# The last four rows of a weight load: one 128-partition DMA, or sixteen of eight partitions

## The chip, the cores and the metric

The kernel runs on one core of a Trainium2 chip. The metric is the device time of one execution in microseconds (us). Before the change it is 186.64 us, the median of three runs (186.52 to 186.93).

## What is computed

One step of attention for 32 sequences, each with one new token, over a cache of which only the last 512 positions are read. There are 32 query heads and 8 key and value heads, each of 128 elements; everything is bf16.

```
q = (x @ wq), reshaped to [32 sequences, 32 heads, 128]          # x 32x512, wq 512x4096
k, v = the last 512 positions of k_cache, v_cache, each head used by 4 query heads
p = softmax(q . k * 128**-0.5)
o = p . v
out = o, reshaped to [32, 4096], @ wo                            # wo 4096x512
```

What has to come from memory is 75.5 MB: wq (4 MB), the windows of both caches (32 MB each, counted in units of 1024 x 1024 bytes) and wo (4 MB).

## The kernel before

The 32 sequences are worked on in eight groups q = 0 to 7 of four. A group's keys (4 MB) and values (4 MB) lie in SBUF across all 128 partitions; there are two buffers for each, `K_sb` and `V_sb`, used in turn. For each group VectorE turns the keys (`T`, L441), TensorE makes the scores (`S`, L331), ScalarE and VectorE the softmax, TensorE multiplies with the values (`P`, L361), and a few small steps bring the result into `o_sel`, the left operand of the output product (`C`, `F`, `D`). The orders of these steps on TensorE, VectorE and ScalarE are written out by hand (L19 to L33).

SyncE (SP) issues all loads but that of x, in the order of `LOADS` (L35): keys and values of the groups, the values of the last three groups in two, two and four pieces (`V_PIECES`, L40), and then wo in three pieces W0, W1 and W2. Four small DMAs for x, of 2, 6, 10 and 14 partitions (`X_PARTS`, L39), are issued by ScalarE at the start (L187).

wo is seen as 128 partitions of 32 rows: partition p holds rows 32p to 32p+31 of the 4096 x 512 matrix, 32 KB in one run in memory. It goes into the buffer of `K_sb[0]`, which is free once VectorE has turned the keys of group 6 (the wait at L240). The pieces are cut along the 32 rows (`WOP`, L41): W0 has rows 0 to 15 of every partition (16 KB each), W1 rows 16 to 27 (12 KB each), W2 rows 28 to 31 (4 KB each, 512 KB in all). Each piece has a semaphore of its own, `sem_wo[j]`, and a DMA adds 16 to it when it is done.

At the end TensorE waits for the last `D` step, and then goes through the pieces in order (L386 to L395): it waits for piece j, and does four matmuls (32 x 128) for each of its rows: 64 for W0, 48 for W1, 16 for W2. All accumulate in one bank, `Y_ps`. VectorE and ScalarE bring that to SBUF (L475, L524), and SP, which has waited for both, issues the one DMA of the output (L248).

Of the kernel before, what the change touches and what calls it, by code (L numbers as in the profile page):

```python
# [38 lines left out]
X_PARTS = [(0, 2), (2, 8), (8, 18), (18, 32)]  # L39
V_PIECES = [1, 1, 1, 1, 1, 2, 2, 4]  # L40
WOP = [(0, 16), (16, 28), (28, 32)]  # L41


def ops_of(text):
    return [(w[0],) + tuple(int(n) for n in w[1:].split(".")) for w in text.split()]


def bass_standalone__sliding_block_cached__sampling_kernel(
# [7 lines left out]
):  # L56
    B, Sq, D = x.shape
    _, HKV, SK, DH = k_cache.shape
    HD = wq.shape[1]
    HQ = HD // DH  # L60
# [3 lines left out]
    P = 128  # L64
# [55 lines left out]
    with ExitStack() as es:  # L120
# [26 lines left out]
        wo_sb = K_sb[0][:, :].rearrange("p (i n) -> p i n", i=NI)  # L147
# [20 lines left out]
        sem_v = [[sem(f"sem_v{i}_{j}") for j in range(max(V_PIECES))] for i in range(2)]  # L168
        sem_wo = [sem(f"sem_wo{i}") for i in range(len(WOP))]
        sem_out = sem("sem_out")  # L170
# [20 lines left out]
        def load_wq(i):  # L191

            nc.sync.dma_start(
                wq_sb[:, 2 * i:2 * i + 2, :].rearrange("p k n -> p (k n)"),
                wq.rearrange("(p k) n -> p k n", k=DKT)[:, 2 * i:2 * i + 2].rearrange("p k n -> p (k n)"),
            ).then_inc(sem_wq[i], 16)
# [4 lines left out]
        def rows(cache, q, r0=0, r1=R):  # L201
            return cache[4 * q:4 * q + 4, :, SK - W:, :].rearrange(
                "b h (k r) d -> (b h) k (r d)", k=KB)[:, :, r0 * DH:r1 * DH]
# [14 lines left out]
        @block.sync  # L218
        def _(sp):
            wait = Waits(sp)  # L220
            load_wq(1)
            wo_r = wo.rearrange("(p i) n -> p i n", i=NI)
            for op in ops_of(" ".join(LOADS)):
                kind, q = op[0], op[1]
                if kind == "K":
                    if q >= 2:
                        wait([ends["T", q - 2, 1]])
                    sp.dma_start(K_sb[q % 2][:, :], rows(k_cache, q)).then_inc(sem_k[q % 2], 16)
                elif kind == "V":
                    if q == 1:  # L230
                        sp.wait_ge(s["pe_q"], 8)
                    if q >= 2:
                        wait([ends["P", q - 2, 31]])
                    n = R // V_PIECES[q]
                    r0 = op[2] * n
                    sp.dma_start(  # L236
                        V_sb[q % 2][:, r0 * DH:(r0 + n) * DH], rows(v_cache, q, r0, r0 + n)
                    ).then_inc(sem_v[q % 2][op[2]], 16)
                else:
                    wait([ends["T", NQ - 2, 1]])  # L240
                    i0, i1 = WOP[q]
                    sp.dma_start(  # L242
                        wo_sb[:, i0:i1, :].rearrange("p i n -> p (i n)"),
                        wo_r[:, i0:i1, :].rearrange("p i n -> p (i n)"),
                    ).then_inc(sem_wo[q], 16)
            sp.wait_ge(s["dve_y"], 2)
            sp.wait_ge(s["act_y"], 2)
            sp.dma_start(  # L248
                out.rearrange("b s n -> b (s n)"), out_sb[:, :, :].rearrange("b c n -> b (c n)")
            ).then_inc(sem_out, 16)  # L250
            sp.wait_ge(sem_out, 16)
# [44 lines left out]
        def _(pe):  # L296
# [87 lines left out]
                run[op[0]](*op[1:]).then_inc(op_sem["PE", op[0]], 1)  # L384
            wait([ends["D", NQ - 1]])
            for j, (i0, i1) in enumerate(WOP):  # L386
                pe.wait_ge(sem_wo[j], 16)
                for i in range(i0, i1):
                    for c in range(4):
                        ins = pe.matmul(  # L390
                            Y_ps[32 * c:32 * (c + 1), 0:P],
                            lhsT=o_sel[:, i, :],
                            rhs=wo_sb[:, i, c * P:(c + 1) * P],
                            start=i == 0, stop=i == NI - 1, tile_position=(0, 32 * c),
                        )  # L395
# [159 lines left out]
```

## Time and profile before

| | us |
|---|---|
| median of three runs | 186.64 |
| the profiled execution's own time | 186.46 |
| span of its profile, first to last instruction | 184.7 |
| VectorE busy | 106.5 |
| TensorE matmul busy | 120.1 |
| ScalarE busy | 49.8 |
| SP issues W0, W1, W2 at | 158.04, 158.69, 159.19 |
| the last TensorE matmul of the kernel ends at | 182.08 |

Times within the profile count from the start of the span, which is 1.76 us shorter than the execution it belongs to. A core's DMAs are carried by 16 DMA engines, and each load by all of them or some of them. A row of a load that lies in one run in memory is one packet in the trace; after the last row that an engine carries of a DMA it writes one packet of 4 bytes, here called a mark, which adds 1 to the DMA's semaphore. The trace has the start and the length of every packet, without the number of its engine, and the time at which every increment of a semaphore landed. Over the span the DMA engines moved 410 GB/s, and the page's row of DMA shares stands at 9 tenths or more from the second of its 40 slices to the 38th.

### The profile page before, as it was taken

How to read it: one execution, taken by the hardware profiler on the slowest of the kernel's cores; microseconds unless marked ns; L12 is line 12 of the kernel's file. 1: busy time of each engine (PE TensorE's matmuls, PEld its weight loads, DVE VectorE, ACT ScalarE, POOL GpSimd, SP SyncE). 2: the span in 40 equal slices, each digit the busy share in tenths (PEclk: the TensorE clock that was granted, in tenths of full speed). 3: DMA queues.
4: the chain of work that ended last, by engine and by line, in shares of the span. 5: the costliest groups of instructions: out<-in, count | busy, mean ns of one | idle time of the engine just before them, and what ended most of it. 6: DMA issues, size and time to landing. Idle time of an engine off the chain costs nothing.

```text
span 184.7 us, 3664 instructions
## 1 busy us (share of the span) xinstructions
PE 120.1 (65%) x1636; PEld 56.9 (31%) x1636; DVE 106.5 (58%) x106; ACT 49.8 (27%) x93; POOL 16.9 (9%) x52
## 2 busy tenths in 40 slices
PE   0089304436599795749944992441899799898942
PEld 0024100013344451403521350000345345354541
DVE  0030999996469632963298327999746996311201
ACT  3000400010952357101650162001072804511211
POOL 7900040201000100002000200010000000000000
PEclk9999955555879999555999699555589999999998
DMA  6999999999999999999999999999999999999970
GB/s 220 411 497 405 405 454 454 447 397 405 451 454 451 390 401 454 454 444 405 392 451 454 440 397 412 454 433 440 415 412 422 419 429 426 410 419 433 425 305 31
DMA packets 3872, 75.80 MB, mean 410 GB/s; under 512 B 464, under 2 KB 528, under 8 KB 656
## 3 DMA queue, kind: packets, MB, share of 16 engines
q1 hardware_dynamic: 3792, 75.53, 96.1%
q8 instruction: 13, 0.21, 0.5%
q10 hardware_dynamic: 64, 0.03, 0.1%
q14 instruction: 3, 0.02, 0.0%
HBM read 75.53 MB, written 0.03 MB: 409 GB/s over the span
## 4 chain that ended last, share of the span: by engine, by line
DMA 59%; DVE 22%; PE 10%; issue 6%; SPq 2%; ACTq 1%; DVEq 0%
DMA K_sb<-in_k_cache_dram 43%; DVE KT_sb L441 16%; DMA K_sb<-in_wo_dram 12%; PE ps L313 4%; PE ps L361 4%; DMA bd<-in_x_dram 4%; DVE QT_sb L433 2%; DVE KT_sb L430 1%; SPq L236 1%; DVE C_sb L466 1%; ACTq L187 1%; SPq L242 1%; PE ps L331 1%; DVE bd L409 0%; PE ps L301 0%
## 5 line engine op out<-in xcount | busy, mean ns | idle before, releaser
L441 DVE STREAM_TRANSPOSE KT_sb<-K_sb 128x4096 f32<-128x4096 f32 x16 | 70.5, 4430 | 10.5 <-DMA K_sb<-in_k_cache_dram 10.4
L361 PE MATMUL ps<-V_sb,bd 32*128 32x512 bf16 x1024 | 63.9, 401 | 4.2 <-DMA V_sb<-in_v_cache_dram 1.6
L331 PE MATMUL ps<-KT_sb,QBD 128*32 128x512 bf16 x256 | 25.1, 529 | 37.3 <-DVE KT_sb L441 28.1
L361 PEld LDWEIGHTS ps<-V_sb,bd 32*128 32x128 bf16 x1024 | 27.3, 98 | 38.5 <-issue 14.9
L331 PEld LDWEIGHTS ps<-KT_sb,QBD 128*32 128x32 bf16 x256 | 6.6, 113 | 52.7 <-DVE KT_sb L441 34.1
L492 ACT ACTIVATE P_f<-ps,negmax 128x512 f32<-128x512 f32 x8 | 5.5, 685 | 60.6 <-DVE negmax L449 60.6
L505 ACT ACTIVATE bd<-PTc,mask 128x512 bf16<-128x512 bf16 x31 | 20.1, 710 | 0.3
L510 ACT ACTIVATE C_sb<-ps 32x512 f32<-32x512 f32 x22 | 12.9, 588 | 25.2 <-PE ps L361 25.1
L289 POOL COPY QBD<-QT_sb 32x128 bf16<-32x128 bf16 x32 | 9.2, 287 | 106.8 <-PE ps L331 89.2
L461 DVE TENSOR_SCALAR bd<-PTc,mask 128x512 bf16<-128x512 bf16 x33 | 9.4, 349 | 14.2 <-ACT PTc L499 14.2
L466 DVE COPY C_sb<-ps 32x512 f32<-32x512 f32 x10 | 6.9, 693 | 14.5 <-PE ps L361 14.3
L373 PE MATMUL ps<-C_sb,F_sb 128*128 128x128 f32 x64 | 10.1, 306 | 7.1 <-ACT C_sb L510 6.5
L373 PEld LDWEIGHTS ps<-C_sb,F_sb 128*128 128x128 f32 x64 | 8.6, 208 | 10.0 <-ACT C_sb L510 8.7
L346 PE MATMUL ps<-P_bf,E_sb 128*128 128x128 bf16 x128 | 10.1, 243 | 0.8 <-DVE P_bf L455 0.8
L313 PE MATMUL ps<-V_sb,bd 128*128 128x512 bf16 x32 | 9.8, 480 | 0.8 <-DVE bd L409 0.8
L346 PEld LDWEIGHTS ps<-P_bf,E_sb 128*128 128x128 bf16 x128 | 8.6, 110 | 4.9 <-DVE P_bf L455 2.8
L447 DVE TENSOR_REDUCE maxv<-ps 128x1 f32<-128x512 f32 x8 | 5.5, 687 | 7.8 <-PE ps L331 7.7
L499 ACT ACTIVATE PTc<-ps 128x512 bf16<-128x512 f32 x8 | 4.8, 594 | 18.5 <-PE ps L346 18.4
L430 DVE CAST KT_sb<-ps 128x512 bf16<-128x512 f32 x4 | 2.5, 684 | 7.3 <-PE ps L313 7.3
L301 PE MATMUL ps<-bd 32*128 32x128 bf16 x4 | 0.6, 295 | 9.0 <-DMA bd<-in_x_dram 9.0
L409 DVE CAST bd<-ps 128x512 bf16<-128x512 f32 x1 | 0.7, 691 | 9.6 <-PE ps L301 9.6
L486 ACT ACTIVATE KT_sb<-ps 128x512 bf16<-128x512 f32 x4 | 2.1, 602 | 15.1 <-PE ps L313 15.1
(29 smaller groups left out, 34.1 us busy)
## 6 DMA issues: line engine op xcount, KB each, us to landing
K_sb<-in_k_cache_dram SPq DMA_DIRECT2D x8, 4096.0 KB, 25.4
V_sb<-in_v_cache_dram SPq DMA_DIRECT2D x5, 4096.0 KB, 29.6
V_sb<-in_v_cache_dram SPq DMA_DIRECT2D x4, 2048.0 KB, 20.5
V_sb<-in_wq_dram SPq DMA_DIRECT2D x2, 2048.0 KB, 9.8
V_sb<-in_v_cache_dram SPq DMA_DIRECT2D x4, 1024.0 KB, 11.6
K_sb<-in_wo_dram SPq DMA_DIRECT2D x1, 2048.0 KB, 18.6
K_sb<-in_wo_dram SPq DMA_DIRECT2D x1, 1536.0 KB, 21.7
K_sb<-in_wo_dram SPq DMA_DIRECT2D x1, 512.0 KB, 22.4
```

The costliest lines, as they stand in the source:

```text
L289: pool.tensor_copy(QBD[pr, q % 2].rearrange("p (w t) (h c) -> p w t h c", w=2, h=HKV)[:, :, :, :, 4 * b:4 * b + 4], QT_sb[pr, q].rearrange ...
L313: ins = pe.matmul(ps[:, n], lhsT=xT_sb[:, kt, :], rhs=wq_sb[:, kt, n * 512:(n + 1) * 512], start=kt == 0, stop=kt == DKT - 1, tile_positio ...
L331: ins = pe.matmul(S_ps[32 * c:32 * c + 32, :], lhsT=QBD[:, q % 2, 2 * w + t, c0:c0 + 32], rhs=KT_sb[:, w, :, KB * h:KB * h + KB, t], start ...
L346: ins = pe.matmul(EP_ps[:, e * R:(e + 1) * R], lhsT=E_sb[:, k, e].rearrange("p m j -> p (m j)"), rhs=P_bf[:, k * R:(k + 1) * R], start=k = ...
L361: ins = pe.matmul(O_ps[:, b, :], lhsT=bd[pr, q % 2, 4 * g:4 * g + 4].rearrange("p r h e -> p (r h e)"), rhs=V_sb[q % 2][pr, 512 * g:512 * ...
L373: ins = pe.matmul(F_ps[:, 0:P], lhsT=F_sb[:, d].rearrange("p h d -> p (h d)"), rhs=C_sb[:, q % 2, :, 32 * d:32 * d + 32], start=d == 0, st ...
L441: return dve.transpose(KT_sb[:, w].bitcast(F32).rearrange("p r c t -> p r (c t)"), K_sb[q % 2][:, :].bitcast(F32).rearrange("p (r w c) -> ...
L447: dve.tensor_reduce(maxv[:, q:q + 1], S_ps, AX.X, ALU.max).then_inc(s["dve_m"], 1)
L461: ins = dve.tensor_scalar(o, i, m, None, op0=ALU.mult)
L466: ins = dve.tensor_copy(*pick_args(q, r))
L505: ins = act.activation(o, i, ACTF.Copy, scale=m)
L510: ins = act.activation(*pick_args(q, r), ACTF.Copy)
```

## The change

W0 and W1 are left as they are. W2 no longer comes by one DMA of 128 partitions but by 16 DMAs of eight partitions: DMA (g, r), with g and r from 0 to 3, takes partitions 32g+r, 32g+r+4, ... 32g+r+28. They are issued by SP in the place of the one DMA, in the order of g and then r, so the first eight cover partitions 0 to 63 and the last eight partitions 64 to 127. Each adds 16 to the same semaphore, and TensorE waits for 256 on it rather than for 16. The bytes, their places and TensorE's work are the same.

```diff
 WOP = [(0, 16), (16, 28), (28, 32)]
+
+WO_ROWS = [128, 128, 8]
...
                     i0, i1 = WOP[q]
-                    sp.dma_start(
-                        wo_sb[:, i0:i1, :].rearrange("p i n -> p (i n)"),
-                        wo_r[:, i0:i1, :].rearrange("p i n -> p (i n)"),
-                    ).then_inc(sem_wo[q], 16)
+                    n = WO_ROWS[q]
+
+                    for p0, step in [(0, 1)] if n == P else [
+                            (32 * g + r, P // (4 * n)) for g in range(4) for r in range(4)]:
+                        pr = slice(p0, p0 + step * (n - 1) + 1, step)
+                        sp.dma_start(
+                            wo_sb[pr, i0:i1, :].rearrange("p i n -> p (i n)"),
+                            wo_r[pr, i0:i1, :].rearrange("p i n -> p (i n)"),
+                        ).then_inc(sem_wo[q], 16)
...
             for j, (i0, i1) in enumerate(WOP):
-                pe.wait_ge(sem_wo[j], 16)
+                pe.wait_ge(sem_wo[j], 16 * (P // WO_ROWS[j]))
```

## Prediction

> **What bounds the kernel now.** I first read the page's DMA part and the end of the chain of waits, because the change touches only the last load. The chain, whose columns are start, length and what, ends so:
>
> ```profile
> 159.19 22.41 DMA K_sb<-in_wo_dram
> 181.60 0.04 issue
> 181.64 0.44 PE ps L390 x16
> 182.08 0.02 issue
> 182.10 0.28 DVE P_bf L475
> ```
>
> The last thing awaited is W2, issued at 159.19 and landed at 181.60. Nothing between 158 and 181.6 but the queue of loads ahead of it holds it up. Next I cut the end into stretches of 1 us and looked at the last two columns, the DMA engines' mean busy share and what they moved:
>
> ```profile
> 176.00:177.00 1.00, 0.98 (x8) 0.78 (x8) 0.00 (x0) 0.00 (x0) 0.00 (x0) 1.00 1.04 426
> 177.00:178.00 1.00, 0.66 (x48) 0.66 (x52) 0.00 (x0) 0.28 (x1) 0.00 (x0) 1.00 0.86 360
> 178.00:179.00 1.00, 0.42 (x32) 0.24 (x20) 0.00 (x0) 0.00 (x0) 0.00 (x0) 1.00 0.63 262
> 179.00:180.00 1.00, 0.00 (x0) 0.00 (x0) 0.00 (x0) 0.00 (x0) 0.00 (x0) 1.00 0.35 143
> 180.00:181.00 1.00, 0.59 (x44) 0.59 (x48) 0.00 (x0) 0.00 (x0) 0.00 (x0) 1.00 0.22 90
> ```
>
> The share falls from 1 to 0.22, about 4 engines of 16, before the load is done: the engines finish far apart, and the end hangs on the last few. The 16 increments of each semaphore, one for each engine, give it exactly (landing times in the trace):
>
> ```
> W1  177.13 .14 .20 .27 .38  .88 .94 178.37   178.66 .74 .95 .98   180.09 .17 .21 .37
> W2  178.32 .38 .42 .51 .62  179.11 .16 .57   179.87 .94 180.15 .20   181.33 .41 .44 .60
> ```
>
> Per engine W2 is 8 rows of 4 KB, 1.2 us after W1. In the packet records a row follows the last by 0.155 us, with 16 engines at work (176.6) and with four (180.7): an engine that falls idle speeds up no other. Four engines are 1.1 us behind the rest. I looked for the cause in the page's queues (packets, MB, share):
>
> ```profile
> q1 hardware_dynamic: 3792, 75.53, 96.1%
> q8 instruction: 13, 0.21, 0.5%
> q10 hardware_dynamic: 64, 0.03, 0.1%
> ```
>
> The 13 packets of q8 are loads of instructions, 16 KB each and 0.96 to 1.10 us long, at 47.4, 58.4, 68.3, 81.6, 93.8, 109.8, 132.5, 141.9, 151.1, 160.5, 167.3, 175.9 and 181.7. Each sets one engine back by about 1.1 us, and it never catches up: after 151.1 one engine's mark of a load is late by that, after 160.5 two, after 167.3 three, after 175.9 four. So eight engines take these loads in turn; four have taken two (the last column of landings) and four one (the third). The other eight had none, and three of them a short load of 8 KB.
>
> **Which engines get W2.** The x loads of 2, 6, 10 and 14 partitions are q10. Its 64 packets are 32 rows and 32 marks, not 4 x 16 marks: a DMA of n < 16 partitions used n engines. So each new DMA takes eight engines, one row each. On a track an engine's next packet starts 4 ns before the last one ends, so I could follow the packets engine by engine. The tracks hold 4, 4, 3, 3, 3, 3, 2, 2, 2, 2, 1, 1, 1, 1, 0, 0 rows of x: the four DMAs used nested sets, the first n of one fixed order. All 16 new DMAs then use the same first eight. The tracks that took the instruction loads of 47.4, 58.4 and 68.3 held 2, 2 and 1 rows of x, so they stand in places 7 to 10, 7 to 10, and 11 to 14. In consecutive places they would be 9, 10, 11 and the fourth 12: the late four, and all eight of these engines, lie in the second half. Later tracks cross too often to be sure of the rest.
>
> [...]
>
> **The sum without any collision.** SP issues 15 more DMAs. The x loads took 0.28 to 0.55 us of issue on ScalarE's queue and W2 0.44 on SP, so the last goes out between 163.7 and 168, and the first engine gets to W2 at 176.6: over 8 us of queued loads hide it. Without that cover each issue would add 0.28 to 0.55. Behind them on SP stands only the output's wait, which ends after 182. Marks: 16 per engine in place of one; a row behind W1's mark starts 6 ns later than one behind a row, and is no longer: 15 x 0.006 = 0.09 us. Fewer marks would be the only gain here, and there are more.
>
> The first half carries 16 rows each, 8 x 0.155 = 1.25 us more. Its latest lands at 179.57 + 1.25 + 0.09 = 180.91. The second half ends with W1, the latest at 180.37, 1.23 earlier than now. W1 is then late next. TensorE has taken (start, length):
>
> ```profile
> 177.34 1.08 PE L390 MATMUL ps<-K_sb,o_sel 128*32 128x128 bf16 x64 [0.37 <-ACT o_sel L514]
> 180.41 0.85 PE L390 MATMUL ps<-K_sb,o_sel 128*32 128x128 bf16 x48 [1.99 <-DMA K_sb<-in_wo_dram]
> 181.64 0.41 PE L390 MATMUL ps<-K_sb,o_sel 128*32 128x128 bf16 x16 [0.38 <-DMA K_sb<-in_wo_dram]
> ```
>
> W1 and W2 in one run are 64 matmuls, 1.08 + 0.03 for the tail that the chain counts in 0.44: 180.37 + 0.04 + 1.11 = 181.52, against 182.08. That would be 0.56 us less. What follows the last matmul is the same.
>
> **The collision.** This takes W2's rows of partitions 64 to 127 from the engines that wrote there and gives them to engines that wrote elsewhere: in a DMA of 128 partitions each engine has eight rows, so two halves of engines serve two sets of partitions. While the late engines still write W1, the first half writes into their partitions. Does that cost? No packet of before shows two big streams into one set. Lower end 0. Upper end: the writes go one after the other, and a late engine loses what its guest writes, up to 8 x 0.155 = 1.25 us. Guests of the early tracks reach the second eight of their rows at 176.6..176.9 + 8 x 0.161 = 177.9..178.2. The late engines' W1 marks are written at 179.65 to 179.91, so they have 1.4 us or more to go: shared evenly, all 1.25 falls on them. A guest of the latest track starts at 177.86 + 1.29 = 179.15 and costs 0.76.
>
> The nearest row is the start, where x goes into partitions 0 to 31 beside wq: the 16 landings of the first wq load come 0.54 us (median, up to 0.65) after their marks were written, those of the key loads after it 0.48. At most 4 KB of x per four partitions is 0.155 us by the upper end; 0.06 to 0.17 was seen. [...]
>
> W1 then lands at 181.34 to 181.62 rather than 180.09 to 180.37. The guests' W2 is in by about 181 to 181.6, in time. TensorE still has all 64 matmuls to do after W1: 181.34..181.62 + 0.04 + 1.11 = 182.49..182.77, so 0.41 to 0.69 us more than 182.08. I take **+0.6**: of the four pairs one has most likely an early guest. From the profiled execution's 186.46 that is 187.06. That execution lies 0.18 below the median shown; against 186.64 it is **187.2**, with 186.9 to 187.5 as this case's own range.
>
> [...]
>
> **The rivals.**
> 1. *No collision*: the sum above, 0.56 less, 185.9 from the profiled run and 186.1 against the median. For it: x rows kept 46 ns and the wq rows beside them 611 ns. Against: the late landings.
> 2. *The wrong half*: the eight instruction-loading engines are every second one (2, 2, 1 fits places 7, 9, 11, 13 as well). One late engine in the first half decides it: its W2 lands at 181.60 + 1.25 + 0.09 = 182.94, TensorE ends at 183.42, 1.34 more: 188.0.
> 3. *A share*: the late engines are served first, or only part collides. W2 of a guest then lands near 181.2 to 181.6: -0.4 to +0.2.
> 4. *It isn't confined*: the 16 DMAs spread over all engines as before. Only the marks cost, 0 to +0.1.
>
> **How the numbers follow.** Collision 0.53 (0.48 slower, 0.05 same); no collision 0.24 (0.22 faster, 0.02 same); wrong half 0.10, slower; a share 0.08 (0.06 same, 0.02 faster); not confined 0.05 (0.04 same, 0.01 slower). A measurement here tells about 0.2% (0.37 us) from no change. Faster 0.24, same 0.17, slower 0.59. Time 187.2. The range reaches down to rival 1 by its lower reading, 185.9, and up to 187.6, the collision's upper end and 0.1; it leaves out the wrong half and little else.
>
> **What would show it.** The semaphore of W2 gets 256 increments, 128 of them long before its data; q1 has 3904 packets (112 more marks). Eight engines end with W1. Right, if W1's last landings come near 181.5 with packets of 12 KB longer than 460 ns from 178 on, and the 64 matmuls run in one piece after them. Wrong, if these stay at 460 ns and W1 lands at 180.4 (rival 1), or if W2 has landings at 182.9 (rival 2). A load of instructions moved by 2 us would also shift which engine is late.

## The result, and the profile after

The changed kernel takes 188.49 us (median of six executions, 187.84 to 189.88), the kernel before beside it 186.75 (186.52 to 187.39): a ratio of 1.0091, with a 95% interval of 1.0062 to 1.0120. It is slower by 1.7 us; 187.2 was forecast, and 187.6 was the upper end. The profiled execution took 189.88 with a span of 188.1: it is the slowest of the six, which has to be kept in mind below. Two executions of later runs were in a slow state of the chip (190.12 in e3_marks, 210.34 in e13_eleven_after), and no median or ratio below counts them.

The end of the chain of waits of the changed kernel, as start, length and what:

```profile
168.76 0.62 SPq L249
...
169.43 15.39 DMA K_sb<-in_wo_dram
184.82 0.04 issue
184.86 0.65 PE ps L397 x16
185.53 0.28 DVE P_bf L482
```

The last thing awaited is still W2, but it lands at 184.82 rather than 181.60. The last of its DMAs goes out at 169.43, long before an engine comes to it (176.6): the issue is hidden. The last 16 matmuls take 0.65 where they took 0.44. TensorE's last instructions, with the idle time ahead of each:

```profile
177.76 1.08 PE L397 MATMUL ps<-K_sb,o_sel 128*32 128x128 bf16 x64 [0.37 <-ACT o_sel L521]
181.54 1.47 PE L397 MATMUL ps<-K_sb,o_sel 128*32 128x128 bf16 x48 [2.69 <-DMA K_sb<-in_wo_dram]
184.86 0.62 PE L397 MATMUL ps<-K_sb,o_sel 128*32 128x128 bf16 x16 [1.86 <-DMA K_sb<-in_wo_dram]
```

W1 comes at 181.49, where the forecast had it (181.34 to 181.62). But the 64 matmuls don't run in one piece: W2 comes 3.3 us later. The stretches of 1 us, whose last three columns are TensorE's granted clock, the DMA engines' share and GB/s:

```profile
178.00:179.00 1.00, 0.84 (x62) 0.67 (x48) 0.00 (x0) 0.00 (x0) 0.00 (x0) 1.00 0.70 262
179.00:180.00 1.00, 0.00 (x0) 0.00 (x0) 0.00 (x0) 0.00 (x0) 0.00 (x0) 1.00 0.60 139
180.00:181.00 1.00, 0.00 (x0) 0.00 (x0) 0.00 (x0) 0.00 (x0) 0.00 (x0) 0.78 0.26 53
181.00:182.00 1.00, 0.46 (x20) 0.47 (x24) 0.00 (x0) 0.00 (x0) 0.00 (x0) 0.50 0.11 41
183.00:184.00 1.00, 0.01 (x3) 0.00 (x0) 0.00 (x0) 0.00 (x0) 0.00 (x0) 0.50 0.03 12
184.00:185.00 1.00, 0.14 (x8) 0.14 (x12) 0.00 (x0) 0.00 (x0) 0.00 (x0) 0.50 0.00 0
```

Three things are to be seen. From 179 to 180 the engines are busy for 0.60 of the time but move 139 GB/s; before, they moved 143 with a share of 0.35. Packets take longer (4 KB rows up to 315 ns, where they took 159): that is the collision, as e1_low will show. From 184 on no engine moves anything, and yet W2 goes on landing until 184.82: data is written, and its marks arrive later. And the clock falls to 0.50 while TensorE waits. The landings themselves, from the semaphores' increments:

```
W1  177.11 .15 .19 .20 .51 .75 .89 178.10   178.70 .84 .88 179.13   181.29 .31 .38 .49
W2  ... 182.97 183.18 .39 .60 .81 184.01 .21 .41 .62 .82
```

The last ten increments of W2 come 0.205 us apart, one engine's marks one after the other; sixteen of them are 3.28 us. In the packet records that engine writes a row and its mark in 0.161 us, and its last row is written at 183.6. Its W1 mark is written at about 180.97, so it is one of the four late engines, and it is among the eight that carry W2. W2's semaphore has 256 increments as forecast, 128 of them long before (16 updates between 160 and 171, one for each DMA), and q1 has the 3904 packets: W2 does go to eight engines.

### The profile page after: what moved, and what is told of

It is laid out like the page before. It is cut to its first block, busy times and chain, and to the rows that moved or that the text cites. A ratio compares the mean times of both kernels' runs of the same rounds, so it can differ in the third digit from the quotient of the medians.

```text
span 188.1 us, 3679 instructions
## 1 busy us (share of the span) xinstructions
PE 119.8 (64%) x1636; PEld 57.8 (31%) x1636; DVE 106.6 (57%) x106; ACT 49.9 (27%) x93; POOL 16.9 (9%) x52
## 3 DMA queue, kind: packets, MB, share of 16 engines
q1 hardware_dynamic: 3904, 75.53, 94.5%
## 4 chain that ended last, share of the span: by engine, by line
DMA 67%; DVE 13%; SPq 8%; issue 6%; PE 5%; DVEq 0%
DMA K_sb<-in_k_cache_dram 59%; DVE KT_sb L448 12%; DMA K_sb<-in_wo_dram 8%; SPq L249 6%; PE ps L368 4%; SPq L238 1%; DVE C_sb L473 1%; PE ps L338 1%; SPq L195 0%; SPq L230 0%; PE ps L397 0%; DVE maxv L454 0%; DVEq L122 0%; DVE P_bf L482 0%; DVE negmax L456 0%
## 5 line engine op out<-in xcount | busy, mean ns | idle before, releaser
L368 PE MATMUL ps<-V_sb,bd 32*128 32x512 bf16 x1024 | 62.5, 394 | 3.9 <-DMA V_sb<-in_v_cache_dram 2.1
L353 PE MATMUL ps<-P_bf,E_sb 128*128 128x128 bf16 x128 | 11.0, 255 | 0.8 <-DVE P_bf L462 0.8
L353 PEld LDWEIGHTS ps<-P_bf,E_sb 128*128 128x128 bf16 x128 | 9.4, 116 | 4.9 <-DVE P_bf L462 2.8
L320 PE MATMUL ps<-V_sb,bd 128*128 128x512 bf16 x32 | 8.6, 436 | 0.8 <-DVE bd L416 0.8
L397 PE MATMUL ps<-K_sb,o_sel 128*32 128x128 bf16 x128 | 3.2, 265 | 4.9 <-DMA K_sb<-in_wo_dram 4.6
L482 DVE CAST P_bf<-ps 32x128 bf16<-32x128 f32 x2 | 0.6, 280 | 9.5 <-PE ps L397 9.5
```

Source lines behind the costliest of these rows:

```text
L320: ins = pe.matmul(ps[:, n], lhsT=xT_sb[:, kt, :], rhs=wq_sb[:, kt, n * 512:(n + 1) * 512], start=kt == 0, stop=kt == DKT - 1, tile_positio ...
L353: ins = pe.matmul(EP_ps[:, e * R:(e + 1) * R], lhsT=E_sb[:, k, e].rearrange("p m j -> p (m j)"), rhs=P_bf[:, k * R:(k + 1) * R], start=k = ...
L368: ins = pe.matmul(O_ps[:, b, :], lhsT=bd[pr, q % 2, 4 * g:4 * g + 4].rearrange("p r h e -> p (r h e)"), rhs=V_sb[q % 2][pr, 512 * g:512 * ...
```

## The theories

The expectations use these letters. **A**, the forecast: writes into the same partitions slow each other. **B**: the many marks or small DMAs slow other loads' rows, wherever they go. **C**, rival 2: a late engine stands among the eight carriers, and it is late through instruction loads. **E**: which engines are late changes from execution to execution. **F**: an engine lands one mark every 0.205 us, whatever the row before it weighs.

All runs, each beside the kernel before (186.71 to 186.82 in the four groups). "Slow rows" are packets over 1.15 times their usual length (159 ns for 4 KB, 460 for 12 KB) near the end; they, the landings and the third column are of the profiled execution:

| run | median | profiled | ratio and 95% interval | last W1 | last W2 | slow rows, 4 KB / 12 KB |
|---|---|---|---|---|---|---|
| the change | 188.49 | 189.88 | 1.0091, 1.0062 to 1.0120 | 181.49 | 184.82 | 28 / 9 |
| e8_again | 188.77 | 189.63 | 1.0096, 1.0064 to 1.0128 | 181.53 | 184.47 | 29 / 8 |
| e1_low | 188.74 | 188.69 | 1.0085, 1.0057 to 1.0113 | 180.49 | 183.53 | 0 / 1 |
| e2_neighbours | 189.28 | 188.62 | 1.0136, 1.0092 to 1.0181 | 182.16 | 183.55 | 107 / 40 |
| e3_marks | 187.15 | 187.24 | 1.0039, 1.0011 to 1.0067 | 180.51 | 181.72 | 0 / 0 |
| e4_two64 | 189.11 | 189.07 | 1.0127, 1.0108 to 1.0145 | 182.23 | 184.01 | 83 / 32 |
| e5_seven | 188.17 | 187.90 | 1.0081, 1.0056 to 1.0106 | 181.32 | 182.84 | 26 / 4 |
| e6_six | 188.01 | 187.90 | 1.0073, 1.0051 to 1.0095 | 181.45 | 182.74 | 28 / 9 |
| e7_high | 189.42 | 189.51 | 1.0143, 1.0124 to 1.0162 | 182.68 | 184.44 | 107 / 37 |
| e9_low_six | 188.69 | 187.19 | 1.0081, 1.0049 to 1.0113 | 180.45 | 182.14 | 0 / 0 |
| e10_fewer_before | 185.20 | 185.23 | 0.9918, 0.9892 to 0.9943 | 179.07 | 180.30 | 0 / 0 |
| e11_fewer_after | 187.33 | 187.18 | 1.0032, 1.0015 to 1.0048 | 178.95 | 182.30 | 4 / 0 |
| e12_low_half | 188.09 | 187.43 | 1.0070, 1.0031 to 1.0109 | 180.37 | 182.51 | no 4 KB rows / 0 |
| e13_eleven_after | 187.94 | 188.96 | 1.0059, 1.0036 to 1.0081 | 180.57 | 183.90 | 0 / 0 |
| e14_fewer_low_half | 187.26 | 187.17 | 1.0023, 1.0006 to 1.0040 | 179.37 | 182.30 | no 4 KB rows / 0 |
| e15_fewer_eight | 185.47 | 186.03 | 0.9919, 0.9888 to 0.9950 | 179.54 | 181.19 | 0 / 0 |

## The experiments

Diffs are against the changed kernel where nothing else is said; `...` stands for lines left out.

### Is it the destination, or the marks? (e1_low, e2_neighbours, e3_marks, e4_two64)

e1_low sends the second eight DMAs to partitions 0 to 63 of an idle buffer, with the same engines, bytes and marks:

```diff
...
+                        to = wo_sb
+                        if p0 >= 64:
+                            p0, to = p0 - 64, other
...
-                            wo_sb[pr, i0:i1, :].rearrange("p i n -> p (i n)"),
+                            to[pr, i0:i1, :].rearrange("p i n -> p (i n)"),
```

> The last eight of the 16 DMAs write the wo rows of partitions 0 to 63 a second time, into the idle keys buffer, so nothing of the last piece goes to partitions 64 to 127 (their four rows of wo are left out of the product). Same bytes, marks, issues and engines. Theory A (guests writing into the partitions of the late engines slow both): no 12 KB packet over 0.5 us after 178, the 4 KB rows stay near 0.159 us, W1 lands by 180.5 as before the change, and W2 on the one late engine of the first eight near 183, span about 186. Theory B (the marks after every row slow all writers, wherever they write): as in the changed kernel, 12 KB packets of 0.9 us, W1 near 181.5, W2 near 185, span 187 to 188.

The slow rows are gone: one 12 KB packet is long, the one beside an instruction load that is long before the change too (964 ns there), and W1 is in at 180.49. So the slow packets of the change come from the destination (A), not from the marks (B). But the time hardly falls. Its two waits of TensorE:

```profile
180.53 1.36 PE L402 MATMUL ps<-K_sb,o_sel 128*32 128x128 bf16 x48 [2.08 <-DMA K_sb<-in_wo_dram]
183.57 0.62 PE L402 MATMUL ps<-K_sb,o_sel 128*32 128x128 bf16 x16 [1.68 <-DMA K_sb<-in_wo_dram]
```

W1 is in time, and W2 still comes 3.0 us after it. In this execution, then, something else than the collision makes most of the loss.

e2_neighbours takes eight neighbouring partitions in each DMA:

```diff
-                            (32 * g + r, P // (4 * n)) for g in range(4) for r in range(4)]:
+                            (n * m, 1) for m in range(P // n)]:
```

> Each of the 16 DMAs takes eight neighbouring partitions in place of every fourth of 32. Same bytes, marks, issues, engines. Theory A (destinations): eight engines write into a narrow set of partitions at once, so the 4 KB rows take 0.3 us or more from the first on, and W2 lands at least 1 us later than in the changed kernel. Theory B (marks): no difference from the changed kernel beyond 0.5 us.

Nearly all W2 rows are slow now, from 177.1 on, up to 333 ns, and the median is 0.8 above the change. W2 of its profiled execution was not later than the change's, against what A would have. The two differ in one thing more, though: 16 marks take 3.28 us, and here W2 lands 1.77 us after the first of the four late landings of W1 (181.78), so no late engine carries W2, as one does in the change's profile.

e3_marks adds 15 small DMAs (8 rows of 64 bytes each) behind W2 of the kernel before, into an idle buffer:

```diff
...
+            for p0 in [32 * g + r for g in range(4) for r in range(4)][:15]:
+                sp.dma_start(
+                    K_sb[1][p0:p0 + 29:4, 0:32], wo_r[p0:p0 + 29:4, 0, 0:32]
+                ).then_inc(sem_tiny, 16)
+            sp.wait_ge(sem_tiny, 16 * 15)
```

> The kernel before with W2 as one DMA, and behind it 15 DMAs of eight partitions of 64 bytes each into the idle keys buffer: the marks and the issues of the change without its bytes. Theory A: W1 and W2 land as before the change (180.4 and 181.6), time within 0.3 us of before. Theory B: the late W1 and W2 packets grow to 0.9 and 0.31 us while the first eight engines write marks, W2 lands 1 us or more later.

No row is slow: B falls. Behind W2 each engine's small marks land 0.2 us apart, the first sight of F. What is left, 0.4 us between the medians and 0.7 by the ratio, is 0.6 us of span in the profile (185.3 against 184.7). Of that the last matmul ends 0.39 later (182.47 against 182.08): TensorE paused 0.63 us between two of W1's matmuls, with an instruction load at 179.6 ahead of it. The other 0.2 is the run's own: SP waits for the added marks as well before it issues the output, the last of them lands at 183.36, and the output goes out at 183.37 rather than at 183.15.

e4_two64 keeps the collision and drops nearly all marks, with W2 as two DMAs of 64 partitions:

```diff
-WO_ROWS = [128, 128, 8]
+WO_ROWS = [128, 128, 64]
-                            (32 * g + r, P // (4 * n)) for g in range(4) for r in range(4)]:
+                            (n * m, 1) for m in range(P // n)]:
```

> W2 by two DMAs of 64 neighbouring partitions, 16 engines with four rows each per DMA: two marks per engine, no load moved between halves of the engines. Theory A: 16 engines write into half the partitions at a time, so rows of 0.2 to 0.32 us appear while all are at W2, and the late engines, nearly alone by then, lose little: W2 lands 0 to 1 us later. Theory B (marks): W2 within 0.2 us of the kernel before.

q1 has 3808 packets, 16 more than before. The end of its chain:

```profile
159.77 24.24 DMA K_sb<-in_wo_dram
184.01 0.04 issue
184.05 0.65 PE ps L397 x16
```

Two DMAs cost 2.4 us, no less than sixteen, and more than A's price: rows of 4 KB take up to 346 ns, and W1 is 1.9 us later than before. Where all of W2's writers meet in one half of the partitions, the collision alone is dear.

### Which engine is late? (e5_seven, e6_six, e7_high, e8_again, e9_low_six)

e5_seven and e6_six take seven and six of each eight partitions, so that the last engines in the order, as the x loads of 2 to 14 partitions showed it, carry nothing of W2; e8_again is the changed kernel in the same group:

```diff
-                        pr = slice(p0, p0 + step * (n - 1) + 1, step)
+                        pr = slice(p0, p0 + step * ((7 if step > 1 else n) - 1) + 1, step)
```

> The 16 DMAs take seven partitions each in place of eight (partitions 28 to 31, 60 to 63, 92 to 95 and 124 to 127 keep old bytes in their last four rows of wo, which are left out of the product). If a DMA of n partitions uses the first n of one fixed order of engines, the eighth engine gets nothing of W2. Theory C (the time comes from one late engine among those that carry W2) with the late one in the eighth place: W2 lands by 182.5 and the time falls to 186.5 to 187.3. With the late one in the seventh place: as the changed kernel, 188 to 189. Theory D (the time comes from the collision alone): 188 or more either way, W1 near 181.5.

> The same with six partitions each (a quarter of the partitions keep old bytes in those rows, left out of the product). Theory C: the late engine gets nothing of W2 whether it stands in place seven or eight, W2 lands by 182.5, time 186.5 to 187.3. If it stands earlier, or under theory D, 188 or more.

> The changed kernel once more, for its spread and a second profile. Theories C and A together: one engine again carries its W2 after a W1 mark near 181, W2 lands between 183 and 185, time 187.8 to 189.9.

The end of e5_seven's chain:

```profile
170.28 12.55 DMA K_sb<-in_wo_dram
182.84 0.04 issue
182.88 0.65 PE ps L397 x9
```

In e8_again W2's last landing, 184.47, comes 3.34 us after the first late landing of W1 (181.13), as the 16 marks of a late engine would have it (C). With seven it comes 1.55 us after it (182.84 and 181.29), with six 1.73 (182.74 and 181.01): none of the late engines has a row of W2. That the late carrier was the eighth in the order, and that leaving it out made the difference, is not shown: e2_neighbours, e7_high and e12_low_half send W2 to eight engines, and none of the late ones carries it there either (1.77, 2.13 and 2.37 us). The median falls by 0.6 and 0.8 from e8_again's, by 0.3 and 0.5 from the change's, in four executions each, and not to the time that C alone would give; W2 is still 1.1 to 1.2 us later than before.

e7_high sends all W2 rows to partitions 64 to 127:

```diff
...
+                        if n < P and p0 < 64:
+                            p0, to = p0 + 64, other
...
```

> All 16 DMAs write to partitions 64 to 127: the first eight put the wo rows of partitions 64 to 127 into the idle keys buffer, the last eight into place (the last four rows of partitions 0 to 63 are left out of the product). Theory A (destinations): the guests collide from their first rows on, so 12 KB packets over 0.5 us appear by 178.3 and not only at 179, W1 lands later than 181.7, W2 later than 185. Theory B (marks): as the changed kernel, W1 181.5 and W2 185.

107 rows are slow, from 177.14 on, and W1 is later by 1.2 us, as A has it. W2 is not later than the change's, which has a late carrier.

e9_low_six joins e1_low and e6_six: without collision and, if the late carrier always stands in place seven or eight, without a late carrier.

> As the run that writes to partitions 0 to 63 alone (upper rows into the idle keys buffer twice over the lower ones), but with six partitions per DMA in place of eight: no guests in partitions 64 to 127, and no W2 on the engine that stood twice behind instruction loads. Left out of the product: the last four rows of wo in partitions 64 to 127 and in a quarter of the others. Theories A and C: both terms gone, W1 lands by 180.5 and W2 by 182.4, time 186.8 to 187.5, so 1.2 to 1.9 below the run with eight partitions. Theory D (collision alone): no gain over that run.

The profiled execution took 187.19, inside what A and C expect together. But seven of eight executions took more, six of them 188.35 to 189.23. An execution of one kernel is not like the next here, which led to E.

### Are instruction loads the cause, and what is left without them? (e10_fewer_before, e11_fewer_after)

Both skip 112 of the 128 value matmuls of groups 0 to 4, in the kernel before and in the changed kernel, so that fewer instructions are loaded:

```diff
+                    if q < 5 and g not in (0, 4, 8, 31):
+                        continue
```

> The kernel before, leaving out 112 of the 128 value matmuls in each of the groups 0 to 4 (the outputs of these groups lack most of their values), so that TensorE has 1120 instructions less and needs 8 or 9 loads of instructions in place of 13. Theory C (an engine's delay is the number of instruction loads that it has carried): at most one engine has carried two when W2 ends, the gap between the last four landings and the rest closes for all but one, W2 lands at 180.2 to 181.6. Rival: the spread of the engines has another cause, and the four late ones stay 1.1 us behind, W2 at 181.6.

> The same shortening of the changed kernel (the same value matmuls left out). Theory C: the W1 landings have no group of four 1.1 us behind, and no stream of W2 rows begins after 180; it is above its own kernel with one DMA for W2 by 0.8 to 1.8 us, for the engines with one load carry 16 rows too. Rival: as much above as the change itself, 1.7 us or more, with one engine's W2 ending after 183.

The queue of instruction loads and the end of the chain of e10_fewer_before:

```profile
q8 instruction: 8, 0.13, 0.3%
```

```profile
160.17 20.13 DMA K_sb<-in_wo_dram
180.30 0.04 issue
180.34 0.44 PE ps L392 x16
```

With eight loads on eight engines none has two, no group of four is 1.1 us late, and W2 is in 1.3 us earlier. The first landing of W1 has not moved (177.20 against 177.13 before), so it is the late group that is gone. The late engines are made by the instruction loads; that part of C is shown. The same end in e11_fewer_after, with three of its stretches of 1 us:

```profile
170.69 11.61 DMA K_sb<-in_wo_dram
182.30 0.04 issue
182.35 0.44 PE ps L399 x16
```

```profile
179.00:180.00 1.00, 0.84 (x48) 0.67 (x48) 0.00 (x0) 0.00 (x0) 0.00 (x0) 1.00 0.43 168
180.00:181.00 1.00, 0.00 (x0) 0.00 (x0) 0.00 (x0) 0.00 (x0) 0.00 (x0) 1.00 0.15 57
181.00:182.00 1.00, 0.00 (x0) 0.00 (x0) 0.00 (x0) 0.00 (x0) 0.00 (x0) 1.00 0.00 0
```

W1 is in at 178.95, with four slow rows in all and no late engine, and the change still costs 2.1 us (187.33 against 185.20), more than was expected. No data moves after 181, and W2 lands at 182.30. So the largest part is neither the collision nor a late engine.

### Bytes or marks? (e12_low_half, e14_fewer_low_half, e15_fewer_eight, e13_eleven_after)

e12_low_half is e1_low with rows of 2 KB:

```diff
-                            to[pr, i0:i1, :].rearrange("p i n -> p (i n)"),
+                            to[pr, i0:i1 if n == P else i0 + 2, :].rearrange("p i n -> p (i n)"),
```

> As the run that writes to partitions 0 to 63 alone, with rows of 2 KB in place of 4 (besides partitions 64 to 127, two of the last four rows of wo are left out everywhere): each of the first eight engines carries as many bytes of W2 as before the change, in 16 rows with 16 marks. If a mark holds up what lands by a fixed 0.05 us, the last engine's landings follow by 0.13 us where its packets follow by 0.09, and W2 lands near 182.4, 0.8 later than before the change; if the hold-up goes with the bytes, by 0.10, and W2 near 181.8.

Half the bytes, and the landings of each of its last two engines still come 0.205 us apart (181.38 .58 .78 .99, and 181.49 .69 .90). The price goes by the mark, not by the byte (F).

e14_fewer_low_half puts the same halved rows into the shortened kernel, and e15_fewer_eight sends only the first eight DMAs, so that each carrier has eight rows and eight marks:

```diff
-                            (32 * g + r, P // (4 * n)) for g in range(4) for r in range(4)]:
+                            (32 * g + r, P // (4 * n)) for g in range(2) for r in range(4)]:
...
```

> Eight instruction loads (112 of 128 value matmuls left out in groups 0 to 4), the 16 DMAs into partitions 0 to 63 alone and with rows of 2 KB (two of the last four rows of wo, and all four in partitions 64 to 127, left out of the product). Theory F (an engine lands a row with its mark every 0.205 us, whatever the row's size): the same time as the changed kernel with eight loads, 187.2 to 187.5, although each engine carries half the bytes. Theory G (the extra bytes cost, marks little): 185.2 to 185.9.

> Eight instruction loads as before, and only the first eight of the 16 DMAs (the last four rows of wo of partitions 64 to 127 are left out of the product): eight rows and eight marks per engine of the first eight. Theory F: 8 x 0.205 in place of 8 x 0.155 for the same bytes as with one DMA, so 0.3 to 0.5 us above the kernel with one DMA and eight loads (185.2), 185.5 to 185.8. Theory G: 185.2 to 185.3.

Their chains end so, e14_fewer_low_half first:

```profile
182.30 0.04 issue
182.34 0.44 PE ps L404 x16
```

```profile
181.19 0.04 issue
181.23 0.44 PE ps L399 x16
```

With half the bytes W2 lands at the same 182.30 as in e11_fewer_after. (The last W1 landing of e14_fewer_low_half, 179.37, stands alone and isn't a carrier's: 16 marks after it would end at 182.65; after the one before it, 179.01, they end at 182.29.) With eight marks it lands at 181.19, and 179.54, where the last carrier's W1 landed, plus 8 x 0.205 = 1.64 is 181.18. F holds, and the median is 0.27 above e10_fewer_before's, 0.03 under the range that F was given.

e13_eleven_after shortens only groups 0 and 1, which leaves 11 loads, no multiple of the eight engines that take them:

```diff
+                    if q < 2 and g not in (0, 4, 8, 31):
+                        continue
```

> The changed kernel, leaving out 112 of the 128 value matmuls in groups 0 and 1 alone, so that TensorE needs 11 or 12 loads of instructions, no multiple of eight. Theory E (the eight engines that load instructions go on in turn from one execution to the next, so which of them are late among those that carry W2 differs between executions): the times spread over 1 us or more, as the changed kernel's 187.8 to 189.9, and not within 0.4 us as with eight loads. Rival: the spread comes from the collisions or from elsewhere in the shortened groups, and this kernel is as narrow as the one with eight loads.

Nine of its ten executions spread over 1.5 us (187.50 to 188.96), where nine of e11_fewer_after's ten lie within 0.43. That speaks for E: with 13 or 11 loads the turn of the eight engines would begin elsewhere in the next execution, and with 8 at the same place. The end of its chain:

```profile
170.48 13.43 DMA K_sb<-in_wo_dram
183.90 0.04 issue
183.95 0.65 PE ps L399 x15
```

Its rows go where the change's go, and not one is slow in this execution; W2 lands at 183.90 all the same, 3.33 us after W1. So the collision isn't given by the destinations alone either. The traces of the kernels with 13 loads and eight carriers bear E out in part: a late engine carries W2 in the change, e8_again and e1_low, and none does in e2_neighbours, e7_high and e12_low_half. e1_low and e12_low_half differ in the size of the rows alone, and the executions of each fall into two groups: 187.14 to 187.83 and 188.51 to 189.17, and 187.27 to 187.50 and 188.68 to 189.04. The profile with the late carrier is from an upper group (188.69), the one without from a lower (187.43). Two traces of one kernel that differ in this are not on record.

## Why the prediction was wrong, step by step

The sign was right and so was W1. The size was 1.7 against 0.6, and the profiled execution's 3.4 us of span comes for the larger part from a term that the forecast had at nearly nothing.

- **"Marks: ... 15 x 0.006 = 0.09 us"** is the step that failed most; with the rows' 1.25 it made 1.34 us for each carrier. It was read from the starts of packets. What releases the wait is the landing of a mark, and an engine lands one in 0.205 us, be it behind a row of 2 KB (e12_low_half) or 4 KB, and in 0.2 behind one of 64 bytes (e3_marks). Sixteen take 3.28 us where eight rows with one mark took 1.23: 2.05 us on every carrier, rows and marks together. For the profiled change, 181.49 + 3.28 = 184.77 against 184.82. It holds where no late engine is left: e11_fewer_after's 2.1 us over e10_fewer_before, with W2 landing 2.00 later.
- **"The first half carries 16 rows each, 8 x 0.155 = 1.25 us more"** is hidden behind the marks: half the bytes save nothing (e14_fewer_low_half). So "the guests' W2 is in by about 181 to 181.6, in time" fails even without a late carrier: e5_seven and e6_six have it at 182.84 and 182.74.
- **"In consecutive places they would be 9, 10, 11 and the fourth 12"** fails too, for the profiled execution of the change: a late engine carries W2 there. That is rival 2, given 0.10; its 182.94 lacked the marks' landings and the collision on that engine. The places had been read from one execution of the kernel before and taken to be the same in all; which place the late carrier had is not shown.
- **The collision** is there, with the packets that were looked for: 313 ns for most of the slow 4 KB rows and up to 912 for 12 KB, in the change and not in e1_low, and W1 at the forecast time. W1's last landing, the late carrier's own, came 181.49 - 180.37 = 1.12 us later (180.49 in e1_low). All four late landings moved so, by 1.1 to 1.2 us (181.29 to 181.49, before 180.09 to 180.37): the size of this term, for which the forecast took its upper end of 1.25 us, was right. But W1 was not what was awaited last, so this mattered through the start of that engine's W2. In the medians its worth can't be seen: e1_low's 188.74 is no less than the change's 188.49 to 188.77. It decides where all writers meet: e4_two64, 2.4 us. What it is in a destination that makes a row take 313 ns rather than 159 is not shown.
- **TensorE** was priced at full clock: 64 matmuls in 1.11. In the change's profile it waited 2.69 us for W1, the clock fell to 0.50, W1's 48 took 1.47 us rather than 0.85, and the last 16 took 0.65, not 0.44.
- **The issue** is hidden, as forecast, though one goes out every 0.66 us, not in 0.28 to 0.55, and the last at 169.43 rather than by 168.

The profiled execution adds up: W2's landing is 184.82 - 181.60 = 3.22 later, of which 1.12 is the collision on the late carrier and 2.05 the marks; with 0.21 for the slow clock that is 3.4. The median's 1.7 is less, and which of these terms is absent from which execution is open. The likeliest reading, E, which the traces bear out in part, is that in some executions no late engine carries W2: then e6_six's profiled 187.90 would be about the time, and the change's fastest took 187.84. Open as well: why one carrier's W1 was set back by writers to partitions 64 to 127 although, by the halves that the forecast took, it carries rows for the first half.

## What to carry to other kernels

Price a small DMA by its marks, one landing after the other on each engine that it uses (here every 0.205 us), and read the landings rather than the packets: the last packet may be written over 1 us before the last mark arrives (183.6 and 184.82 in the change). A row given to an engine that falls idle can slow both if it goes to partitions that others still write to (in the change 4 KB rows of 313 ns rather than 159 and 12 KB rows of up to 912 rather than 460; in e13_eleven_after none). Where an end hangs on a few late engines, find what made them late before moving work around them; here fewer instructions, not another split of the load, brought 1.5 us (e10_fewer_before, which leaves out work).

## What the runs showed of the hardware

- An engine landed one mark every 0.205 us behind back-to-back small DMAs, for rows of 2 KB (e12_low_half) and 4 KB (the change) alike, and every 0.2 us for rows of 64 bytes (e3_marks), though it wrote a row and mark of 4 KB in 0.161 us. Whether the semaphore write itself or something ahead of it takes the 0.205 us is not shown.
- SP took 0.62 us to issue eight strided partitions (the change), 0.30 for eight neighbouring ones (e2_neighbours) and 0.43 to 0.60 for all 128 (W0, W1 and W2).
- TensorE's granted clock fell to 0.50 at 180.57 in the change, in a wait that had begun at 178.85. In e2_neighbours it was still 1.00 from 182 to 183, after a wait of 3.35 us, and in e7_high W1's 48 matmuls took 1.09 us after a wait of 4.27, between the 0.85 of the kernel before and the 1.47 of the change. How long a wait lowers it is not shown.
